# Loading the second chunk's q two tokens to a row and turning it by heads and parity

## The chip, the cores and the metric

The kernel runs on one core of one Trainium2 chip. The metric is the device time of one execution in microseconds (us); smaller is better. Before the change the median of three runs is 208.63 us.

## The reference

Two layers follow each other. The first is a linear attention with decay, in blocks of 64 tokens, over 4 batches, 8 heads, 768 tokens and a head width of 64. The second is a feed-forward layer whose activation is h + sin(alpha h)^2 / alpha, on 3072 tokens of width 512 with an inner width of 2048.

```python
for b in range(nb):                                   # blocks of 64 tokens
    intra = einsum('bhic,bhjc->bhij', qb, kb) * Dmask
    intra = einsum('bhij,bhjd->bhid', intra, vb)
    inter = einsum('bhid,bhde->bhie', qb * lam_pow, kv_state)
    out[:, :, sl] = intra + inter
    kv_state = lam_block * kv_state + einsum('bhsd,bhse->bhde', kb * rev_pow, vb)
x = out.transpose(0, 2, 1, 3).reshape(B * S, H * D)
h = x @ w_in
s = sin(alpha * h)
result = (h + s * s / (alpha + 1e-9)) @ w_out
```

All inputs and the output are fp32; the kernel computes with bf16 operands on TensorE.

## The kernel before

The 768 tokens are cut into six chunks `t` of 128 tokens, each with all four batches, which gives groups `g` of 512 rows for the feed-forward layer. While group `g` goes through the feed-forward layer, the attention of chunk `g + 1` is worked in between. The order of all instructions is written by hand: the program text is the order on every engine. TensorE makes 16 hidden blocks `f` of a group (`hidden`, L461: four matmuls of 512 columns each) and, in units of four matmuls, the second product (`project`, L489). Such units wait in the list `behind` and are put in by `run(n)`. ScalarE computes the sine and mostly the square (L464, L469; for some blocks of group 0 the square is on VectorE, L477). VectorE finishes a block (`finish`, L478).

For the attention of chunk 1, which the change is about, these steps matter:

- Loads. GpSimd issues them; they convert fp32 to bf16. Each row that is read is one token of one head, 64 values. A load puts the 128 tokens on 128 partitions, with 16 rows (two batches times eight heads) side by side on each (`load`, L104). For q and k of batches 2 and 3, the heads of the pair stand one place further (L101 and L102), in two transfers.
- Turning. Scores need q and k with the head width on partitions. `turn` makes four transposes on TensorE for one batch (two heads at a time, L281) into one PSUM bank, and a copy brings them to the tile `QKT`: on ScalarE (L283) or VectorE (L285). k of chunk 1 is turned by `turns_pair` (L295, L298). Later chunks are turned mostly by the DMA.
- `scores` (L397) multiplies turned k and q into two banks, `masks` (L404, VectorE) applies the decay, and `states` (L377) makes the key-value products. `update` adds these to the state on VectorE (L353, L357); GpSimd decays and casts states (L342, L346), and `decay_k` (L242, GpSimd) makes the decayed k.
- `outputs_first` (L411) multiplies q by the state, `outputs` (L436) adds the scores times v, and `leave` (L443, VectorE) writes the attention's result.

Around the first turn of q the text runs as follows. It names the banks in use, which sets what waits for what:

```python
        if f == 13:
            turn(1, "q", 0, 2, V)        # bank 2
            turn(1, "q", 1, 3, V)        # bank 3
        if f == 14:
            scores(1, (0,), (4, 2))      # banks 4 and 2
            masks(1, 0)
        if f == 15:
            run(1)
            states(1, (0,), (4, 2))      # the same banks
```

The second turn of q, for batches 2 and 3, comes after group 0's hidden blocks: into banks 5 and 0, copied by ScalarE, followed by one unit of `project` (the first that reads the third part of w_out) and `scores(1, (1,), (5, 0))`. Banks 5 and 0 hold `outputs_first` of the first pair before, which `leave` reads.

Of the kernel before, what the change touches and what calls it, by code (L numbers as in the profile page):

```python
# [11 lines left out]
BF16 = mybir.dt.bfloat16  # L12
# [3 lines left out]
def kernel(  # L16
# [11 lines left out]
    nc = tc.nc  # L28
    P = nc.NUM_PARTITIONS

    B, H, S, D = q.shape
    T = 128
    NT = S // T
    HP = H // 2
# [23 lines left out]
    def bank(nm, n, dtype=FP32):  # L58
        return psum.tile([P, 512 if dtype is FP32 else 1024], dtype, name=nm, tag=f"b{n}")
# [6 lines left out]
    LO, HI = slice(0, D), slice(D, 2 * D)  # L66
# [4 lines left out]
    qn, kn, vn = {}, {}, {}  # L71
    NAT = {"k": (kn, k), "q": (qn, q), "v": (vn, v)}

    def new_chunk(t):
        for d, nm, p in ((qn, "qn", qkp), (kn, "kn", qkp), (vn, "vn", vp)):
            d[t] = p.tile([P, B, H, D], BF16, name=nm)
# [14 lines left out]
    def load_w_out(i):  # L91
        nc.gpsimd.dma_start(out=w_out_sb[i][:],
                            in_=moe_w_out[i * 512:(i + 1) * 512, :].rearrange("(f p) d -> p f d", p=P))

    def load(t, nm, b0, b1):
        dst, src = NAT[nm]
        to = dst[t][:, b0:b1, :, :].rearrange("p b h e -> p (b h) e")
        by_head = src[b0:b1, :, t * T:(t + 1) * T, :].rearrange("b h p e -> p (b h) e")
        n = H * (b1 - b0)
        if t and nm != "v" and b0 == 2:  # L100
            nc.gpsimd.dma_start(out=to[:, 0:n - 1, :], in_=by_head[:, 1:n, :])  # L101
            nc.gpsimd.dma_start(out=to[:, n - 1:n, :], in_=by_head[:, 0:1, :])  # L102
        else:
            nc.gpsimd.dma_start(out=to, in_=by_head)  # L104

    new_chunk(0)
    new_chunk(1)
# [24 lines left out]
    iden = consts.tile([P, P], BF16, name="iden")  # L132
# [71 lines left out]
    def mask_table():  # L204
        nc.gpsimd.tensor_tensor(
            out=C64[:], in0=tri64[:].unsqueeze(1).unsqueeze(1).broadcast_to([P, 2, HE, D]),
            in1=later["NE64"][:].unsqueeze(3).broadcast_to([P, 2, HE, D]), op=ALU.mult)


    V, G, A = nc.vector, nc.gpsimd, nc.scalar  # L210
    xt = {}
    kdec = {}
    KT, QT, both = {}, {}, {}
# [14 lines left out]
    def home(t, blk):  # L228
        return SB[2 if blk else t % 2]
# [7 lines left out]
    def decay_k(t, b0, b1):  # L237
        if t not in kdec:
            kdec[t] = kdp.tile([P, B, H, D], BF16, name="kdec")
        R = later["R64" if t else "R128"]  # L240
        o = int(turned_by_one(t, b0 // 2))
        nc.gpsimd.tensor_tensor(out=kdec[t][:, b0:b1, :, :], in0=kn[t][:, b0:b1, :, :],  # L242
                                in1=R[:, o:o + H].unsqueeze(1).unsqueeze(3).broadcast_to([P, b1 - b0, H, D]),
                                op=ALU.mult)
# [32 lines left out]
    def turn(t, nm, b, n, eng):  # L277
        src, u = (kn, 0) if nm == "k" else (qn, 1)
        ps = bank("T_ps", n, BF16)[:].rearrange("p (n c i) -> p n c i", n=2, c=HP)[:, u]
        for hp in range(HP):  # L280
            nc.tensor.transpose(out=ps[:, hp, :], in_=src[t][:, b, 2 * hp:2 * hp + 2, :], identity=iden[:])  # L281
        if eng is nc.scalar:
            eng.copy(out=both[t][:, u, b, :, :], in_=ps)  # L283
        else:
            eng.tensor_copy(out=both[t][:, u, b, :, :], in_=ps)  # L285

    def halves(hd):
        return slice(hd * D, (hd + 1) * D)

    def turns_pair(t, nm, b, bk, engines):  # L290
        src, n = (kn, 0) if nm == "k" else (qn, 1)
        ps = bank("T_ps", bk, BF16)[:].rearrange("p (u c i) -> p u c i", u=2, c=HP)
        for u in range(2):
            for hp in range(HP):
                nc.tensor.transpose(out=ps[:, u, hp, :], in_=src[t][:, b + u, 2 * hp:2 * hp + 2, :], identity=iden[:])  # L295
        for u, eng in enumerate(engines):
            if eng is nc.scalar:
                eng.copy(out=both[t][:, n, b + u, :, :], in_=ps[:, u])  # L298
            else:
                eng.tensor_copy(out=both[t][:, n, b + u, :, :], in_=ps[:, u])  # L300

    def scores1(t, b, ns):
        Fb = [bank("F0_ps", n)[:].rearrange("p (c i) -> p c i", c=HP) for n in ns]
        for hp in range(HP):
            for hd in range(2):
                nc.tensor.matmul(out=Fb[hd][:, hp, :], lhsT=KT[t][halves(hd), b, hp, :],
                                 rhs=QT[t][halves(hd), b, hp, :], start=True, stop=True)
        st = work.tile([P, 2, HP, T], BF16, name="STm")
        for hd in range(2):
            nc.vector.tensor_tensor(out=st[:, hd], in0=Fb[hd], in1=C0[:, hd], op=ALU.mult)  # L310
        STm[t, b] = st
# [18 lines left out]
    def states1(t, pr, n):  # L330
        ps = bank("KV0_ps", n)[:].rearrange("p (u c d) -> p u c d", u=2, c=HP)
        for h in range(2 * H):
            half, m = where(1, pr, h)
            nc.tensor.matmul(out=ps[halves(half), m // HP, m % HP, :], lhsT=head(kdec, t, pr, h),
                             rhs=vn[t][:, 2 * pr + h // H, h % H, :], start=True, stop=True)
        new_state(1, pr, ps, "first")
# [4 lines left out]
    def decay_state(n, pr):  # L341
        nc.gpsimd.tensor_tensor(out=pair(SD, pr), in0=pair(S_of[n], pr), op=ALU.mult,  # L342
                                in1=L64[:, pr].unsqueeze(1).unsqueeze(3).broadcast_to([P, 2, HP, D]))

    def cast_state(n, pr, dst):
        nc.gpsimd.tensor_copy(out=pair(dst, pr), in_=pair(S_of[n], pr))  # L346
# [54 lines left out]
    def masks(t, pr):  # L401
        st = work.tile([P, 2, 2, HP, D], BF16, name="STm")
        for hd in range(2):
            nc.vector.tensor_tensor(out=st[:, hd], in0=att["F", t, pr, hd], op=ALU.mult,  # L404
                                    in1=of_mask(C64, t, pr, hd).unsqueeze(1).broadcast_to([P, 2, HP, D]))
        STm[t, pr] = st
# [50 lines left out]
    def hidden(g, f, between=None):  # L457
        hps = bank("hps", H0[f] if g == 0 else (0, 5, 4, 2)[f] if g == 1 and f < 4 else AB[0] if g == 1 and f == 15 else AB[f + 1] if g == 2 and f < 2 else HB[(f + 2) % 3] if g == 1 else HB[(16 * g + f + 1) % 3])
        w = w_in_sb[f // 4]
        for c in range(NDC):  # L460
            nc.tensor.matmul(out=hps[:], lhsT=w[:, c, (f % 4) * P:(f % 4 + 1) * P],  # L461
                             rhs=xt[g][:, c, :], start=(c == 0), stop=(c == NDC - 1))
        s_sb = mlps.tile([P, GRP], BF16, name="s_sb")
        nc.scalar.activation(out=s_sb[:], in_=hps[:], func=ACTF.Sin, scale=alpha_sb[:, f:f + 1])  # L464
        if between:
            between()
        s2 = mlps.tile([P, GRP], BF16, name="s2")
        if squarer(g, f) is A:
            nc.scalar.activation(out=s2[:], in_=s_sb[:], func=ACTF.Square)  # L469
        elif squarer(g, f) is G:  # L470
            nc.gpsimd.tensor_tensor(out=s2[:], in0=s_sb[:], in1=s_sb[:], op=ALU.mult)
        hps_of[g, f] = (hps, s_sb, s2)
# [102 lines left out]
    decay_k(0, 0, 2)  # L575
    decay_k(0, 2, 4)
    mask_table()
    for nm in "kqv":
        load(1, nm, 0, 2)
    load_w_out(1)  # L580
    for nm in "kv":
        load(1, nm, 2, 4)
# [20 lines left out]
    def run(n):  # L603
        for _ in range(min(n, len(behind))):
            behind.pop(0)()
# [3 lines left out]
    for f in range(NFC):  # L609
        hidden(0, f)  # L610
        if f in (1, 10):
            states1(0, f // 10, 2 if f == 10 else 4)
        if f == 10:
            decay_k(1, 0, 2)
            decay_state(1, 0)
            cast_state(1, 0, home(1, 0))
            load(1, "q", 2, 4)
            load_w_out(2)
            load_w_out(3)
            load(2, "v", 0, 2)  # L620
        if f in (11, 12):
            run(1)
        if f == 12:
            turns_pair(1, "k", 0, 4, (A, A))
        if f == 13:
            turn(1, "q", 0, 2, V)
            turn(1, "q", 1, 3, V)
        if f == 14:
            scores(1, (0,), (4, 2))
            masks(1, 0)  # L630
        if f == 15:
            run(1)
            states(1, (0,), (4, 2))
            finish(0, 14)
            update(1, 0, 0)
        if f != 14:
            finish(0, f)
# [3 lines left out]
    update(1, 1, 0)  # L641
    run(2)
    turns_pair(1, "k", 2, 4, (A, A))
    run(1)
    outputs_first(1, (0,), (5, 0))
# [4 lines left out]
    states(1, (1,), (4, 2))  # L650
    update(1, 0, 1)
    run(1)
    turn(1, "q", 2, 5, A)
    turn(1, "q", 3, 0, A)
    load(2, "k", 0, 2)
    run(1)
    update(1, 1, 1)
# [110 lines left out]
```

## Time and profile before

| | before |
|---|---|
| median of 3 runs | 208.63 us (208.5 to 208.82) |
| the profiled execution's own time | 209.41 us |
| its span in the trace | 207.6 us |
| TensorE busy | 198.1 us (95%) |
| VectorE busy | 131.5 us (63%) |
| ScalarE busy | 142.8 us (69%) |
| GpSimd busy | 108.7 us (52%) |

The trace is of one execution. Its times count from the start of the span. In the rows PE is TensorE's matmuls, PEld its weight loads, DVE VectorE, ACT ScalarE and POOL GpSimd. L281 is line 281 of the kernel. A row of the timeline gives the start, the time from the first start to the last end, the engine, the line and the operation, what is written and read with its shape, and the count of instructions merged. In brackets stands the idle time before it, and what ended that. A few matmul records are missing, so a group of four can show as three.

### The profile page before, as it was taken

To read this page: it belongs to the slowest core of one execution; us is meant where nothing else is said; L and a number is where in the kernel's file an instruction comes from. 1 tells how busy PE (TensorE), PEld (TensorE's weight loads), DVE (VectorE), ACT (ScalarE), POOL (GpSimd) and SP (SyncE) were. 2 spreads that over 40 slices of the span, in tenths; PEclk is the share of its full clock that TensorE was granted. 3 is DMA by queue.
4 is the path that set the end of the run, shared out by engine and by line. 5 is a ranking of instruction groups with operands and counts; after the bars stand their busy time and mean duration, and the time that the engine had idled before them with its cause. 6 is when DMAs were issued, how large, how long until landed. Compare 5 with 4: busy or idle time off the path is not lost.

```text
span 207.6 us, 5321 instructions
## 1 busy us (share of the span) xinstructions
PE 198.1 (95%) x2203; PEld 98.7 (48%) x2233; DVE 131.5 (63%) x218; ACT 142.8 (69%) x240; POOL 108.7 (52%) x114
## 2 busy tenths in 40 slices
PE   7996999999999999999999999999999999999993
PEld 2652445564455445444444444444445444444462
DVE  6792898582898969967556957555867544444000
ACT  4895998323989799675776575776666787887121
POOL 8999949998799984999966930002000000000000
PEclk9999999999999999999999999999999999999999
DMA  8999999999999999699999999501101101110212
GB/s 127 148 151 203 197 164 182 175 188 157 124 215 191 150 138 200 51 163 159 109 139 151 181 124 163 143 0 54 51 3 54 51 0 51 52 54 0 101 61 92
DMA packets 98826, 24.47 MB, mean 118 GB/s; under 512 B 91490, under 2 KB 95858, under 8 KB 98802
## 3 DMA queue, kind: packets, MB, share of 16 engines
q0 software_dynamic: 77248, 13.37, 88.7%
q1 hardware_dynamic: 21552, 10.76, 26.9%
q8 instruction: 17, 0.28, 0.6%
q14 instruction: 7, 0.06, 0.1%
q10 hardware_dynamic: 2, 0.00, 0.0%
HBM read 27.27 MB, written 6.29 MB: 162 GB/s over the span
## 4 chain that ended last, share of the span: by engine, by line
PE 67%; DMA 14%; POOL 11%; issue 3%; ACT 3%; DVE 0%; POOLq 0%; ACTq 0%; SPq 0%
PE ops L489 30%; PE hps L461 29%; DMA qn<-in_q_dram 6%; DMA QKT<-qn 5%; DMA w_in<-in_moe_w_in_dram 3%; POOL vn L104 2%; ACT s_sb L464 2%; PE O_ps L411 2%; POOL kn L104 2%; POOL qn L104 2%; PE hps L513 2%; POOL SD L342 2%; PE F_ps L397 1%; POOL sb L346 1%; PE O_ps L436 1%
## 5 line engine op out<-in xcount | busy, mean ns | idle before, releaser
L478 DVE SCALAR_TENSOR_TENSOR gall<-s,r_sb,hps 128x512 bf16<-128x512 bf16 x96 | 71.1, 744 | 45.1 <-ACT s L469 44.9
L461 PE MATMUL hps<-xt,w_in 128*128 128x512 bf16 x369 | 94.4, 379 | 2.8 <-DMA w_in<-in_moe_w_in_dram 1.7
L489 PE MATMUL ops<-w_out,gall 128*128 128x512 bf16 x353 | 90.3, 379 | 1.0 <-issue 0.3
L464 ACT ACTIVATE s_sb<-hps,alpha_sb 128x512 bf16<-128x512 f32 x96 | 65.3, 684 | 33.6 <-PE hps L461 33.1
L469 ACT ACTIVATE s<-s_sb 128x512 bf16<-128x512 bf16 x91 | 57.3, 630 | 2.8
L461 PEld LDWEIGHTS <-w_in 128*128 128x128 bf16 x384 | 36.5, 98 | 44.8 <-DMA w_in<-in_moe_w_in_dram 2.5
L489 PEld LDWEIGHTS <-gall 128*128 128x128 bf16 x368 | 34.8, 98 | 40.6 <-issue 0.8
L242 POOL TENSOR_TENSOR kdec<-kn,R 128x1024 bf16<-128x1024 bf16 x12 | 23.0, 1943 | 5.4 <-DMA kn<-in_k_dram 5.4
L346 POOL CAST sb<-S 128x512 bf16<-128x512 f32 x20 | 12.3, 620 | 20.7 <-DVE S L353 20.7
L342 POOL TENSOR_TENSOR SD<-S,L 128x512 f32<-128x512 f32 x16 | 16.7, 1047 | 6.2 <-DVE S L353 6.0
L443 DVE TENSOR_TENSOR xt<-O_ps,Etab 128x512 bf16<-128x512 f32 x20 | 12.8, 684 | 6.3 <-PE O_ps L436 6.3
L104 POOL DMA_DIRECT2D vn<-in_v_dram x13 | 14.8, 1152 | 0.0
L496 DVE COPY o_sb<-ops 128x512 f32<-128x512 f32 x15 | 10.3, 689 | 4.2 <-PE ops L489 4.1
L404 DVE TENSOR_TENSOR STm<-F_ps,C 128x512 bf16<-128x512 f32 x20 | 12.8, 681 | 0.2 <-PE F_ps L397 0.2
L498 ACT COPY o_sb<-ops 128x512 f32<-128x512 f32 x8 | 4.6, 576 | 12.0 <-PE ops L489 12.0
L353 DVE TENSOR_TENSOR S<-SD,KV_ps 128x512 f32<-128x512 f32 x16 | 10.9, 682 | 0.2 <-POOL SD L342 0.2
L130 PE MATMUL hps<-fill 128*128 128x256 bf16 (+1 forms) x30 | 8.3, 386 | 1.5 <-DVE fill L123 1.5
L104 POOL DMA_DIRECT2D kn<-in_k_dram x8 | 8.8, 1106 | 0.3 <-issue 0.3
L104 POOL DMA_DIRECT2D qn<-in_q_dram x8 | 8.7, 1091 | 0.0
L283 ACT COPY QKT<-T_ps 128x512 bf16<-128x512 bf16 x10 | 5.5, 586 | 3.4 <-PE T_ps L281 3.2
L101 POOL DMA_DIRECT2D qn<-in_q_dram x5 | 6.1, 1221 | 1.3 <-DMA qn<-in_q_dram 1.3
L411 PEld LDWEIGHTS <-sb 64*64 64x64 bf16 x320 | 4.4, 108 | 4.8 <-issue 4.7
(75 smaller groups left out, 114.0 us busy)
## 6 DMA issues: line engine op xcount, KB each, us to landing
out_dram<-o_sb SPq DMA_DIRECT2D x23, 256.0 KB, 2.3
vn<-in_v_dram POOLq DMA_DIRECT2D x10, 256.0 KB, 8.8
w_out<-in_moe_w_out_dram POOLq DMA_DIRECT2D x4, 512.0 KB, 11.0
w_in<-in_moe_w_in_dram POOLq DMA_DIRECT2D x3, 512.0 KB, 10.3
kn<-in_k_dram POOLq DMA_DIRECT2D x5, 256.0 KB, 8.4
qn<-in_q_dram POOLq DMA_DIRECT2D x5, 256.0 KB, 10.1
kn<-in_k_dram POOLq DMA_DIRECT2D x5, 240.0 KB, 8.3
qn<-in_q_dram POOLq DMA_DIRECT2D x5, 240.0 KB, 9.0
```

What stands on the lines that cost most here:

```text
L104: nc.gpsimd.dma_start(out=to, in_=by_head)
L242: nc.gpsimd.tensor_tensor(out=kdec[t][:, b0:b1, :, :], in0=kn[t][:, b0:b1, :, :], in1=R[:, o:o + H].unsqueeze(1).unsqueeze(3).broadcast_to ...
L342: nc.gpsimd.tensor_tensor(out=pair(SD, pr), in0=pair(S_of[n], pr), op=ALU.mult, in1=L64[:, pr].unsqueeze(1).unsqueeze(3).broadcast_to([P, ...
L346: nc.gpsimd.tensor_copy(out=pair(dst, pr), in_=pair(S_of[n], pr))
L353: nc.vector.tensor_tensor(out=S, in0=pair(SD, pr), in1=ps, op=ALU.add)
L404: nc.vector.tensor_tensor(out=st[:, hd], in0=att["F", t, pr, hd], op=ALU.mult, in1=of_mask(C64, t, pr, hd).unsqueeze(1).broadcast_to([P, 2 ...
L443: nc.vector.tensor_tensor(out=xview(t)[:, 2 * pr:2 * pr + 2, blk, :, :], in0=att["O", t, pr, blk], in1=Eb, op=ALU.mult)
L461: nc.tensor.matmul(out=hps[:], lhsT=w[:, c, (f % 4) * P:(f % 4 + 1) * P], rhs=xt[g][:, c, :], start=(c == 0), stop=(c == NDC - 1))
L464: nc.scalar.activation(out=s_sb[:], in_=hps[:], func=ACTF.Sin, scale=alpha_sb[:, f:f + 1])
L469: nc.scalar.activation(out=s2[:], in_=s_sb[:], func=ACTF.Square)
L478: nc.vector.scalar_tensor_tensor(out=gall[g][:, f, :], in0=s2[:], scalar=r_sb[:, f:f + 1], in1=hps[:], op0=ALU.mult, op1=ALU.add)
L489: nc.tensor.matmul(out=ops[:], lhsT=gall[g][:, f, m * P:(m + 1) * P], rhs=w_out_sb[part][:, f % 4, :], start=(f == 0), stop=(f == NFC - 1))
```

## The change

Only q of chunk 1 is touched. A row that is read now holds two neighbouring tokens of a head, 128 values. A batch's 128 tokens lie on 64 partitions: the first batch of a pair on the lower half, the second on the upper half. On each partition are eight heads, each with the even and then the odd token of its pair of tokens. The load of batches 0 and 1 is two transfers instead of one. That of batches 2 and 3 is three instead of two, as the second half is split by the shift of heads.

Turning takes 16 transposes for a pair of batches, one for each head place and parity: 128 partitions and 64 columns go to 64 partitions and 128 columns. The columns of a result are 64 token pairs of the one batch and 64 of the other. All 16 go to one bank, where a pair took two banks before. The heads alternate between the lower and the upper half of the partitions. Then two copies, one for each batch, write tokens back in order: even and odd tokens go to every second element of `QKT`. The first pair's copies are on VectorE and the second pair's on ScalarE, as before.

```diff
+    def in_twos(t, b):
+        return qn[t][:, b:b + 2].rearrange("p b h d -> p (b h d)").rearrange("p (h x) -> p h x", h=H)
+
+    def load_twos(t, b):
+        src = q[b:b + 2, :, t * T:(t + 1) * T, :].rearrange("b h (p e) d -> p (b h) (e d)", e=2)
+        o = int(bool(t) and b == 2)
+        for rows, s0, s1, n in ((LO, 0, H, o), (HI, 0, H - o, H + o), (HI, H - o, H, 0)):
+            if s0 < s1:
+                nc.gpsimd.dma_start(out=in_twos(t, b)[rows, s0:s1, :], in_=src[:, n:n + s1 - s0, :])
...
+    def turn_twos(t, b, bk, engines):
+        ps = bank("T_ps", bk, BF16)[:].rearrange("p (c e n) -> p c e n", c=HP, e=2)
+        for s in range(H):
+            for e in range(2):
+                nc.tensor.transpose(out=ps[halves(s % 2), s // 2, e, :],
+                                    in_=in_twos(t, b)[:, s, e * D:(e + 1) * D], identity=iden[:])
+        for u, eng in enumerate(engines):
+            to = both[t][:, 1, b + u, :, :].rearrange("p c (i e) -> p c e i", e=2)
+            if eng is nc.scalar:
+                eng.copy(out=to, in_=ps[:, :, :, u * D:(u + 1) * D])
+            else:
+                eng.tensor_copy(out=to, in_=ps[:, :, :, u * D:(u + 1) * D])
...
-    for nm in "kqv":
-        load(1, nm, 0, 2)
+    load(1, "k", 0, 2)
+    load_twos(1, 0)
+    load(1, "v", 0, 2)
...
-            load(1, "q", 2, 4)
+            load_twos(1, 2)
...
-            turn(1, "q", 0, 2, V)
-            turn(1, "q", 1, 3, V)
+            turn_twos(1, 0, 2, (V, V))
...
-    turn(1, "q", 2, 5, A)
-    turn(1, "q", 3, 0, A)
+    turn_twos(1, 2, 5, (A, A))
```

## The prediction

> **What bounds the kernel now.** I read the page's head first, then the windows view for the stretch in which chunk 1 is turned, then the timelines of TensorE, VectorE, ScalarE and GpSimd there.
>
> ```profile
> span 207.6 us, 5321 instructions
> PE 198.1 (95%) x2203; PEld 98.7 (48%) x2233; DVE 131.5 (63%) x218; ACT 142.8 (69%) x240; POOL 108.7 (52%) x114
> ```
> ```profile
> 30.00:50.00 20.00, 19.49 (x347) 10.91 (x352) 13.73 (x27) 8.83 (x17) 19.54 (x21) 1.00 1.98 176
> ```
>
> TensorE is busy for 95% of the span, and for 19.49 of the 20 us around the change, at full granted clock (the 1.00). Only 0.51 us of idle time is there to win. So what counts is whether the change lengthens TensorE's stream or puts a wait into it. TensorE's rows around the first turn (q of batches 0 and 1, at hidden block 13):
>
> ```profile
> 31.77 1.03 PE L461 MATMUL hps<-xt,w_in 128*128 128x512 bf16 x3
> 32.63 0.61 PE L281 MATMUL T_ps<-iden,qn 128*128 128x128 bf16 x8
> 33.08 1.03 PE L461 MATMUL hps<-xt,w_in 128*128 128x512 bf16 x4
> 34.03 0.45 PE L397 MATMUL F_ps<-QKT 64*64 64x64 bf16 x32
> 34.41 0.82 PE L461 MATMUL hps<-xt,w_in 128*128 128x512 bf16 x3
> 35.28 1.03 PE L489 MATMUL ops<-w_out,gall 128*128 128x512 bf16 x4
> 36.24 0.45 PE L377 MATMUL KV_ps<-vn,kdec 64*64 64x64 bf16 x32
> 36.62 1.90 PE L489 MATMUL ops<-w_out,gall 128*128 128x512 bf16 x8
> ```
>
> Columns: start, length, engine, line, operation. A group of four 512-column matmuls takes 0.86 us of issue (35.28 to 36.14; "x3" rows lack a record). The groups follow each other without a gap, except that 0.1 us passes before a group of 64-wide tiles (36.14 to 36.24). VectorE in the same stretch, and one earlier row for a price:
>
> ```profile
> 29.29 0.68 DVE L351 COPY S<-KV_ps 128x512 f32<-128x512 f32 x1
> 33.05 0.76 DVE L285 COPY QKT<-T_ps 128x512 bf16<-128x512 bf16 x2 [0.27 <-PE T_ps L281]
> 33.77 0.42 DVE L477 TENSOR_TENSOR s<-s_sb 128x512 bf16<-128x512 bf16 x1
> 34.23 0.75 DVE L478 SCALAR_TENSOR_TENSOR gall<-s,r_sb,hps 128x512 bf16<-128x512 bf16 x1
> 34.89 1.28 DVE L404 TENSOR_TENSOR STm<-F_ps,C 128x512 bf16<-128x512 f32 x2
> ```
>
> From the q copies (L285) to the end of the masks (L404, 36.17) VectorE has no slack: the square and finish of block 13 stand between them. And the key-value products (L377) at 36.24 write the two banks that the masks read. They come 0.07 us after the masks end. So here TensorE is one step ahead of a VectorE chain that is just in time; whatever delays the copies moves TensorE.
>
> **Part 1: the transposes.** Each pair of batches goes from 8 transposes of 128 columns of q to 16 of 64 columns; the identity still streams 128 columns. No row shows a transpose with a 64-column result. The nearest are the 128-wide transposes and L317, which has the same shape (128 rows, 64 result columns, 128 streamed):
>
> ```profile
> L281 PE MATMUL T_ps<-iden,qn x32: 216/219/311, 6.5 to 43.4; 128*128 128x128 bf16 x32
> L317 PE MATMUL O_ps<-STm,vn x32: 219/219/243, 12.7 to 14.8; 128*64 128x128 bf16 x32
> 12.74 0.64 PE L317 MATMUL O_ps<-STm,vn 128*64 128x128 bf16 x16
> 13.31 0.50 PE L130 MATMUL hps<-fill 128*128 128x256 bf16 x3
> ```
>
> Taking the last one's 0.219 us off the group, the 8 transposes start (0.61 - 0.219)/7 = 56 ns apart, and L317's 16 start (0.64 - 0.219)/15 = 28 ns apart: its results alternate between the two halves of the partitions, and two run at once. The next group starts 0.15 us after L317's last start (13.16 to 13.31). The new loop also changes halves, but only after two instructions (the parities) on the same half. If one half works while the other is issued, 28 ns holds on average too. Bounds: 28 and 56 ns. I take 28, the row of the same shape. First turn: start 32.63 + 0.1, last start 0.42 later (33.15), its end 33.37 (high end: 33.57 and 33.79). The next group starts at 33.30 instead of 33.08.
>
> **Part 2: the copies on VectorE.** Both copies now read one bank, so the first waits for all 16 transposes; before, it waited for the first four. It starts at 33.40 instead of 33.05 (the same 0.03 us after the last end). Each still moves 512 elements per partition, but writes every second 2-byte element. No row shows that. The nearest rows are L285 itself (0.42 each, 0.76 for two) and L351, the copy of as many fp32 elements (0.68; two of that length take 1.28, by L404). L285 saves 0.26 us, half a nanosecond an element: it seems to move two neighbours at a time. Outputs two apart are not neighbours, so I take L351's: 1.28 us. It cannot be below 0.76, since no element is saved.
>
> The Trainium skill's page "VectorE: DVE Perf Modes", section "What auto-detection actually checks", says that the paired 16-bit mode needs a step of one in every tensor, and so speaks against this change. By its table in "The TRN2 errata" a 512-element copy out of PSUM would be an estimated 658 ns unpaired and 392 paired; with these the sum would differ by 0.01 us.
>
> Ends: 33.40 + 1.28 = 34.68 instead of 33.81, so 0.87 late. The square, finish and masks follow, all 0.87 later; masks end at 37.04, and L377 starts at 37.11 instead of 36.24: **0.87 us**. TensorE's own path asks for less: scores (L397) wait for the copies until about 34.73 instead of 34.03 (0.70), so L377 would be there at 36.94 and wait 0.17 for the masks. Low end, paired copies: 0.35. High end, 56 ns: 1.29. Behind L377 everything on TensorE moves with it.
>
> **Part 3: the second turn** (q of batches 2 and 3):
>
> ```profile
> 39.76 0.69 PE L411 MATMUL O_ps<-QKT,sb 64*64 64x64 bf16 x31
> 42.92 0.68 PE L281 MATMUL T_ps<-iden,qn 128*128 128x128 bf16 x8
> 43.63 1.02 PE L489 MATMUL ops<-w_out,gall 128*128 128x512 bf16 x4
> 44.59 0.55 PE L397 MATMUL F_ps<-QKT 64*64 64x64 bf16 x32
> 44.95 0.78 PE L411 MATMUL O_ps<-QKT,sb 64*64 64x64 bf16 x31
> 43.34 1.07 ACT L283 COPY QKT<-T_ps 128x512 bf16<-128x512 bf16 x2 [2.65 <-PE T_ps L281]
> 43.89 1.12 DVE L357 SCALAR_TENSOR_TENSOR S<-S,L,KV_ps 128x128 f32<-128x128 f32 x4
> ```
>
> In the old times: transposes from 43.02, last start 43.44, so the next group can start at 43.59, no later than now (43.63): the 8 took 0.71 us from start to the next group, 0.26 more than in the first turn, since the second four waited for bank 0. The new form uses bank 5 only. But both ScalarE copies now wait for the last transpose: 43.69 instead of 43.34. Two take 1.07, which I keep (low and high end alike, as ScalarE's copies are 0.58 whether they write 2 or 4 bytes by the row below), until 44.76. Scores write bank 5 and must wait for both, to 44.80 instead of 44.59: 0.21 late. Of this 0.09 comes back, since L411 behind them takes 0.78 here and 0.69 at 39.76, held by the state update (L357, until 45.01), which will be done. Net **0.12 us**; with 56 ns, 0.54.
>
> ```profile
> 49.82 0.58 ACT L498 COPY o_sb<-ops 128x512 f32<-128x512 f32 x1 [3.81 <-PE ops L489]
> ```
>
> **Part 4: the loads.** Rows of the queue and of landing times (first issue of q at 21.37; then w_out 2; then w_out 0):
>
> ```profile
> 21.37 1.25 POOL L104 DMA_DIRECT2D qn<-in_q_dram  x1
> 30.46 1.89 POOL L242 TENSOR_TENSOR kdec<-kn,R 128x1024 bf16<-128x1024 bf16 x1 [3.02 <-DMA kn<-in_k_dram]
> 33.86 1.26 POOL L101 DMA_DIRECT2D qn<-in_q_dram  x1
> 35.11 0.58 POOL L102 DMA_DIRECT2D qn<-in_q_dram  x1
> DMA to landing us min/median/max: 10.2/10.5/10.8
> DMA to landing us min/median/max: 7.9/7.9/7.9
> DMA to landing us min/median/max: 13.9/13.9/13.9
> ```
> ```profile
> DMA packets 2458, 0.31 MB, mean 156 GB/s; under 512 B 2458, under 2 KB 2458, under 8 KB 2458
> DMA packets 828, 0.82 MB, mean 206 GB/s; under 512 B 23, under 2 KB 828, under 8 KB 828
> ```
>
> The first of these two windows (28 to 30 us) is q, k and v: 128-byte packets, 2 x 16/2458 us = 13.0 ns of an engine each. The second (19 to 23) is 1-KB weight rows, 77 ns each. Between them 256 bytes cost 22 ns: q of two batches falls from 2048 x 13.0/16 = 1.67 us to 1024 x 22/16 = 1.41. That is 0.26 us a load (none if bytes alone count, 0.83 if packets alone do), and TensorE sees none of it: q lands at 21.37 + 10.8 = 32.17 and is used at 32.63. GpSimd issues one transfer more each time. By L101 and L102 (1.26 for 15 rows per partition, 0.58 for one) a half of 64 partitions and 8 rows is about 0.7: 1.4 instead of 1.25, then 2.0 instead of 1.84. The first is hidden in the 3.02 us in which L242 waits for k. In the program the transfers take turns on eight semaphores, so one more moves the last v load behind w_out 0's landing, 28.4 us; it ends by 29.6, still ahead of L242. If that cover fails, it costs what passes 30.46. The second 0.2 us lies ahead of a state cast that will itself come later with TensorE. I cost both at nothing.
>
> **Sum.** 0.87 + 0.12 = 0.99 us. Against the profiled execution: span 207.6 to 208.6, its own time 209.41 to 210.4; that run lies 0.78 above the median 208.63 of three, so the median goes to 209.6. Bounds: 0.35 + 0.12 = 0.47, so 209.1; 1.29 + 0.54 = 1.83, so 210.5.
>
> **Rivals.**
> - Paired copies: VectorE keeps 0.42 a copy with every second element written. For it: nothing but the equal count; against it: the 0.26 that L285 saves needs an explanation. 209.1.
> - Transposes one by one, 56 ns: two in a row on the same half block the next pair. For it: L317 alternates every instruction, this doesn't. 210.5.
> - Late q: 64 partitions reach only half of the DMA engines. Then 1024 x 22/8 = 2.8 us instead of 1.67, q lands at 33.3, transposes start 0.6 to 0.7 later than the 32.73 above: 1.65 in all, 210.3. Against it: nothing in the trace splits engines by partition. It decides once q lands after 32.7.
> - Faster: the shorter loads free TensorE from waits on the queue. w_out 2 lands at 35.67 + 7.9 = 43.57, and L489 starts on it at 43.63 though the transposes were all issued by 43.4. If that and the rest of the 0.51 us of idle time went, and transposes and copies came no later, 208.1. It decides only if copies come less than about 0.1 us late; the sixteen starts and the shared bank speak against that. If the loads' packets don't grow at all, the first forecast stands, since it takes nothing from them.
>
> **How the numbers follow.** This kernel's times can be told apart by about 0.2%, 0.42 us. Chances: the sum 0.52; paired copies 0.18 (0.05 of it within 0.2%, as 209.1 is near the edge of 209.05); one by one 0.14; late q 0.07; relief 0.09 (0.06 faster, 0.03 within). Slower 0.86, same 0.08, faster 0.06. The range runs from 209.0 (below paired copies) to 210.4 (late q and part of one by one); it leaves out relief and the far end of one by one.
>
> **What would show it.** Right: 16 transposes whose last starts 0.42 us after the first; VectorE copies of 0.68; masks ending 0.9 later relative to block 13; L377 waiting for them; scores of the second turn 0.2 late; no load row on TensorE's waits. Wrong: copies of 0.42, starts 56 ns apart, a wait of the first transposes for q, or TensorE's lost time made up behind 45 us, where I see no slack.

## The result and the profile after

| | before | with the change |
|---|---|---|
| median | 208.72 us (6 runs, 208.44 to 209.07) | 209.97 us (6 runs, 209.37 to 210.74) |
| ratio to before | | 1.0056, 95% interval 1.0032 to 1.0081 |
| ratio when run again with the experiments | | 1.0038, 1.0019 to 1.0057 |
| the profiled execution's own time | 209.41 us | 209.37 us |
| its span | 207.6 us | 207.6 us |

Two comparisons put the change 0.6% and 0.4% slower, about 1.2 and 0.8 us. The two traced executions have the same span all the same: the one of before, 209.41 us, is slower than all six runs in the table, and the one with the change is the fastest of its six. So the traces must be compared by stages, not by their ends. Two later traces, of the loads alone and of the repeated change, were taken at a granted clock of 0.56 and 0.66 and are left aside. TensorE's rows of the changed kernel around the two turns of q (L316 the transposes, L420 scores, L400 key-value products, L434 `outputs_first`, L484 hidden blocks, L512 `project`):

```profile
31.00 1.03 PE L484 MATMUL hps<-xt,w_in 128*128 128x512 bf16 x4
31.96 0.64 PE L316 MATMUL T_ps<-iden,qn 128*64 128x128 bf16 x16
32.53 1.04 PE L484 MATMUL hps<-xt,w_in 128*128 128x512 bf16 x4
33.52 0.19 PE L420 MATMUL F_ps<-QKT 64*64 64x64 bf16 x1
34.04 0.44 PE L420 MATMUL F_ps<-QKT 64*64 64x64 bf16 x31 [0.33 <-DVE QKT L323]
36.24 0.51 PE L400 MATMUL KV_ps<-vn,kdec 64*64 64x64 bf16 x32
43.09 0.64 PE L316 MATMUL T_ps<-iden,qn 128*64 128x128 bf16 x16
43.78 1.02 PE L512 MATMUL ops<-w_out,gall 128*128 128x512 bf16 x4
45.15 0.45 PE L420 MATMUL F_ps<-QKT 64*64 64x64 bf16 x32 [0.34 <-ACT QKT L321]
45.43 0.67 PE L434 MATMUL O_ps<-QKT,sb 64*64 64x64 bf16 x31
51.72 1.03 PE L512 MATMUL ops<-w_out,gall 128*128 128x512 bf16 x4
```

And the copies on VectorE and ScalarE with what follows the first pair, from the timelines:

```profile
32.65 1.34 DVE L323 COPY QKT<-T_ps 128x512 bf16<-128x512 bf16 x2 [0.62 <-PE T_ps L316]
33.88 0.40 DVE L500 TENSOR_TENSOR s<-s_sb 128x512 bf16<-128x512 bf16 x1
34.98 1.28 DVE L427 TENSOR_TENSOR STm<-F_ps,C 128x512 bf16<-128x512 f32 x2
43.77 1.33 ACT L321 COPY QKT<-T_ps 128x512 bf16<-128x512 bf16 x2 [3.01 <-PE T_ps L316]
```

In the changed trace two rows now name a wait of the scores for a copy (34.04 and 45.15). From the start of hidden block 13 to the key-value products it takes 36.24 - 31.00 = 5.24 us; before it took 36.24 - 31.77 = 4.47. That is 0.77 more. From there to the `project` group between the hidden blocks of group 1 it takes 15.48 (to 51.72), before 15.11 (to 51.35, the row below): 0.37 more. Of this, 0.07 lies in the key-value products themselves: the next group follows 0.45 after their start (36.69), before 0.38. I call the whole stretch, 19.58 us before and 20.72 after, **the stage**. It is 1.14 us longer.

Two things outside the stage give that back in these two traces. The first weights let TensorE go on at 17.50 instead of 18.27. And in chunk 4 the unchanged kernel waited for a turn by the DMA, which the changed one did not. Rows of before, then of after:

```profile
18.27 1.04 PE L461 MATMUL hps<-xt,w_in 128*128 128x512 bf16 x4 [1.72 <-DMA w_in<-in_moe_w_in_dram]
51.35 1.03 PE L489 MATMUL ops<-w_out,gall 128*128 128x512 bf16 x4
116.22 0.45 PE L397 MATMUL F_ps<-QKT 64*64 64x64 bf16 x32
116.89 0.45 PE L397 MATMUL F_ps<-QKT 64*64 64x64 bf16 x32 [0.23 <-DMA QKT<-qn]
117.27 1.04 PE L489 MATMUL ops<-w_out,gall 128*128 128x512 bf16 x3
```
```profile
17.50 1.04 PE L484 MATMUL hps<-xt,w_in 128*128 128x512 bf16 x4 [1.19 <-DMA w_in<-in_moe_w_in_dram]
116.58 0.74 PE L420 MATMUL F_ps<-QKT 64*64 64x64 bf16 x64
117.25 1.04 PE L512 MATMUL ops<-w_out,gall 128*128 128x512 bf16 x4
```

The first of the two lies ahead of every changed instruction. It scatters: in the twelve traces compared here, hidden block 13 began between 30.99 and 31.80 us. The second is not there every time: a second trace of the kernel before, from the experiments below, has no such wait:

```profile
31.54 1.03 PE L461 MATMUL hps<-xt,w_in 128*128 128x512 bf16 x3
51.47 1.03 PE L489 MATMUL ops<-w_out,gall 128*128 128x512 bf16 x4
116.33 0.74 PE L397 MATMUL F_ps<-QKT 64*64 64x64 bf16 x64
117.00 1.04 PE L489 MATMUL ops<-w_out,gall 128*128 128x512 bf16 x3
```

Its stage is longer, 19.93 us. But from block 13 to the `project` unit behind these scores both traces of the kernel before take the same, 85.50 (to 117.27) and 85.46 (to 117.00), and the change takes 86.25 (to 117.25). So the 1.14 us of the stage is the larger of two readings. Against the second trace the stage is 0.79 us longer, and over the longer stretch the change costs 0.75 to 0.79.

### The profile page after: what moved, and what is told of

Its sections match the earlier page's. It is cut to its first block, busy times and chain, and to the rows that moved or that the text cites. A ratio compares the mean times of both kernels' runs of the same rounds, so it can differ in the third digit from the quotient of the medians.

```text
span 207.6 us, 5386 instructions
## 1 busy us (share of the span) xinstructions
PE 199.6 (96%) x2249; PEld 97.9 (47%) x2249; DVE 132.0 (64%) x218; ACT 143.1 (69%) x240; POOL 109.3 (53%) x116
## 4 chain that ended last, share of the span: by engine, by line
PE 89%; POOL 5%; DMA 3%; ACT 1%; issue 1%; DVE 0%; POOLq 0%; ACTq 0%
PE hps L484 40%; PE ops L512 39%; DMA w_in<-in_moe_w_in_dram 3%; PE O_ps L434 2%; PE F_ps L420 2%; PE hps L536 2%; PE KV_ps L400 2%; POOL kn L104 1%; PE O_ps L459 1%; POOL qn L104 1%; POOL vn L104 1%; POOL vn L126 1%; PE T_ps L305 1%; ACT QKT L321 1%; PE T_ps L316 1%
## 5 line engine op out<-in xcount | busy, mean ns | idle before, releaser
L484 PE MATMUL hps<-xt,w_in 128*128 128x512 bf16 x384 | 95.9, 379 | 1.3 <-DMA w_in<-in_moe_w_in_dram 1.2
L512 PE MATMUL ops<-w_out,gall 128*128 128x512 bf16 x368 | 92.1, 379 | 0.1
L487 ACT ACTIVATE s_sb<-hps,alpha_sb 128x512 bf16<-128x512 f32 x96 | 65.3, 685 | 33.3 <-PE hps L484 33.1
L484 PEld LDWEIGHTS <-w_in 128*128 128x128 bf16 x384 | 36.5, 98 | 44.4 <-DMA w_in<-in_moe_w_in_dram 2.0
L512 PEld LDWEIGHTS <-gall 128*128 128x128 bf16 x368 | 34.8, 98 | 40.6 <-issue 0.6
L140 PE MATMUL hps<-fill 128*128 128x256 bf16 (+1 forms) x30 | 7.6, 360 | 1.5 <-DVE fill L133 1.5
L104 POOL DMA_DIRECT2D kn<-in_k_dram x8 | 8.8, 1101 | 0.3 <-issue 0.3
L104 POOL DMA_DIRECT2D qn<-in_q_dram x7 | 7.4, 1062 | 0.0
L434 PEld LDWEIGHTS <-sb 64*64 64x64 bf16 x320 | 4.3, 108 | 4.8 <-issue 4.2
L101 POOL DMA_DIRECT2D kn<-in_k_dram x5 | 6.3, 1258 | 0.0
L434 PE MATMUL O_ps<-QKT,sb 64*64 64x64 bf16 x320 | 5.7, 195 | 0.0
```

The source lines that it names most:

```text
L434: nc.tensor.matmul(out=att["O", t, pr, blk][halves(h % 2), u, h // 2, :], lhsT=home(t, blk)[halves(half), 2 * pr + m // HP, m % HP, :], rh ...
L512: nc.tensor.matmul(out=ops[:], lhsT=gall[g][:, f, m * P:(m + 1) * P], rhs=w_out_sb[part][:, f % 4, :], start=(f == 0), stop=(f == NFC - 1))
```

## The experiments

All were compared with the kernel before in the same session. "Stage" is as above, from one trace each; that of the loads alone is from their second trace. With the loads alone, the turning alone or dense copies, the tokens of chunk 1's q end up in another order, so these kernels show times only.

| edit | ratio, 95% interval | stage, us |
|---|---|---|
| the kernel before again | 0.9997, 0.9974 to 1.0020 | 19.93 |
| the loads of the change alone | 1.0059, 1.0032 to 1.0085 | 20.84 |
| the turning of the change alone | 1.0052, 1.0027 to 1.0078 | 20.73 |
| the change, dense copies | 1.0046, 1.0023 to 1.0069 | 21.00 |
| the loads alone, v later | 0.9988, 0.9964 to 1.0011 | 20.02 |
| the change, dense copies, v later | 1.0019, 0.9993 to 1.0045 | 20.19 |
| the change, v later | 1.0043, 1.0015 to 1.0072 | 20.72 |
| the change in two banks, v later | 1.0017, 0.9993 to 1.0042 | 20.35 |
| the kernel before, v later | 0.9995, 0.9976 to 1.0013 | 20.20 |
| the kernel before, TensorE 0.76 us late | 1.0019, 0.9998 to 1.0040 | 20.35 |

**Loads or turning.** The first theory was that the turning costs the time and the loads cost nothing; the rival, that GpSimd's additional transfers do.

```diff
 # loads alone: the change, but
-            turn_twos(1, 0, 2, (V, V))
+            turn(1, "q", 0, 2, V)
+            turn(1, "q", 1, 3, V)
-    turn_twos(1, 2, 5, (A, A))
+    turn(1, "q", 2, 5, A)
+    turn(1, "q", 3, 0, A)
 # turning alone: the change, but
-    load_twos(1, 0)
+    load(1, "q", 0, 2)
-            load_twos(1, 2)
+            load(1, "q", 2, 4)
```

> Only the loads of the change; q is turned as before, from 64-partition rows, so the tokens and batches of chunk 1's q are mixed up in its result. Stage measured: from the first matmul of hidden block 13 to the project group behind the two hidden blocks of group 1, 19.58 us before (31.77 to 51.35), 20.72 with the change (31.00 to 51.72). If the turning and its copies cost the time: stage 19.4 to 19.6, whole 208.4 to 208.8. If the loads do (one more transfer each time on GpSimd, v held back behind the weights): stage above 20.2, whole above 209.3.

> Only the turning of the change; q is loaded as before, so its tokens are mixed up in the result. If the turning and its copies cost the time: stage 20.6 to 20.8, whole 209.7 to 210.1. If the loads do: stage 19.6 to 19.9, whole below 209.1.

The turning alone costs all that the change costs (stage 20.73), as expected. But so do the loads alone: 1.0059, against my expectation. The new theory was tested on a second trace of the loads alone:

> The loads alone once more (token order of chunk 1's q wrong), for a trace at full clock. New theory: the extra transfer makes GpSimd wait for an earlier transfer ahead of the second chunk's v load, and the state casts behind it come late. Then the first cast behind that load starts 0.7 to 1.1 us later than 38.28 - 31.77 = 6.51 after hidden block 13, O_ps waits for it, and the stage is 20.0 to 20.4 instead of 19.58. If GpSimd has slack, as I predicted: 19.4 to 19.6.

TensorE and GpSimd of that trace, from the timelines:

```profile
32.51 0.61 PE L291 MATMUL T_ps<-iden,qn 128*128 128x128 bf16 x8 [0.19 <-DMA qn<-in_q_dram]
36.83 1.90 PE L512 MATMUL ops<-w_out,gall 128*128 128x512 bf16 x8
44.62 0.41 PE L420 MATMUL F_ps<-QKT 64*64 64x64 bf16 x21
45.75 0.28 PE L420 MATMUL F_ps<-QKT 64*64 64x64 bf16 x11 [0.72 <-issue]
45.84 0.67 PE L434 MATMUL O_ps<-QKT,sb 64*64 64x64 bf16 x31
```
```profile
28.21 1.16 POOL L104 DMA_DIRECT2D vn<-in_v_dram  x1 [1.71 <-DMA w_out<-in_moe_w_out_dram]
39.21 0.63 POOL L369 CAST sb<-S 128x512 bf16<-128x512 f32 x1
44.96 0.62 POOL L369 CAST sb<-S 128x512 bf16<-128x512 f32 x1
```

The new theory held in part: the casts are late, but not in the place that I named. The first cast behind the v load is 7.91 us after hidden block 13 (39.21 - 31.30; expected 7.2 to 7.6, before 6.51), but `outputs_first` of the first pair did not wait for it, as it starts at 39.97. The next cast, at 44.96, ends at 45.58, and `outputs_first` of the second pair needs it: it starts at 45.84, instead of right behind the scores. Why the last eleven score products stop with it, the profile doesn't name. The first turn also waited 0.35 us for q (32.51 instead of 32.16). So the stage, 20.84, is above the expected 20.0 to 20.4, and the casts are only part of it: of the 1.26 us over 19.58, 0.58 lies behind the key-value products (15.31 us from 36.83 to the end of the stage, before 14.73) and 0.68 ahead of that, where q was late.

**The v loads moved.** To take the casts away as a cause, the two v loads of chunk 2 that stand ahead of them are issued later.

```diff
-            load(2, "v", 0, 2)            # behind the w_out loads, hidden block 10
...
-    load(2, "v", 2, 4)
+    load(2, "v", 0, 2)
...
+    load(2, "v", 2, 4)                    # behind update(1, 0, 1)
     load(2, "k", 0, 2)
```

> The loads alone (token order wrong), with the two v loads of chunk 2 issued later: the first where the second stood, the second behind the state update of the second pair. If the casts behind the first v load are what the loads cost: no wait of O_ps for a cast, stage back to 19.4 to 19.6, whole within 0.2% of before. If the loads cost in another way: stage as in the run without this move, whole 0.4% above before.

> The whole change, only with the two v loads of chunk 2 later. If late casts and late copies are two chains side by side, of which the later one counts, then taking the casts away alone leaves the copies: stage 20.5 to 20.7 us, whole 0.3 to 0.5% above before. If they add up: stage 19.6 to 20.0, whole within 0.2% of before.

> The kernel before with only the two v loads of chunk 2 issued later. If GpSimd's casts held TensorE a little even before (O_ps at 44.95 took 0.78 instead of 0.69): ratio 0.998 to 1.000, stage 19.4 to 19.6. If they had slack: ratio 1.000, stage 19.6 to 19.9.

With the loads alone the move takes the cost away: 0.9988. The stage is 20.02; what is left over 19.58 lies in the first turn, where VectorE's chain was late, and in no cast: behind the key-value products it takes 14.72 us, before 14.73. This execution began late, with block 13 at 31.76, and did not wait for q, so its stage shows the casts gone and no late q. The fall of the ratio, from 1.0059 to 0.9988, is larger than 0.58 us; for the rest the traces do not account. On the whole change the move takes little or nothing: 1.0043, stage 20.72. So the loads' late casts and the turning's late copies lie side by side, and only the later one counts; they don't add. On the kernel before the move does nothing that these runs can tell: 0.9995. Its stage of 20.20 was longer than I expected either way, and its row says why (kernel before, v later):

```profile
43.75 0.59 PE L489 MATMUL ops<-w_out,gall 128*128 128x512 bf16 x2 [0.82 <-DMA w_out<-in_moe_w_out_dram]
```

Here hidden block 13 began early, at 31.07, and TensorE then waited at the first use of w_out's third part.

**Dense copies.** The copies write neighbours, which leaves the tokens in another order.

```diff
-            to = both[t][:, 1, b + u, :, :].rearrange("p c (i e) -> p c e i", e=2)
+            to = both[t][:, 1, b + u, :, :].rearrange("p c (e i) -> p c e i", e=2)
```

> The change with the four copies writing neighbours: even and odd tokens stay apart, so the token order of chunk 1's turned q is wrong. If the copies' length is the main cost: VectorE's copies fall from 0.72 to 0.42 and ScalarE's from 0.74 to 0.58, and the stage from 20.7 to 20.0 to 20.2 us, whole about 209.2 to 209.4. If the sixteen transposes on TensorE are: stage 20.6 to 20.7, whole unchanged against the change.

> The change with dense copies (token order wrong) and the two v loads of chunk 2 later. If the dense copies saved time on TensorE's stream and the late casts took it back: stage 20.0 to 20.3 instead of 21.00 with dense copies alone, and 20.72 for the change. If it stays above 20.6, copies and casts are not the cause.

The copies' rows, of the change first and of dense copies then (the lines' view: minimum, median and maximum in ns):

```profile
L323 DVE COPY QKT<-T_ps x2: 708/720/731, 32.6 to 33.3; 128x512 bf16<-128x512 bf16 x2
L321 ACT COPY QKT<-T_ps x2: 736/736/736, 43.8 to 44.4; 128x512 bf16<-128x512 bf16 x2
```
```profile
L323 DVE COPY QKT<-T_ps x2: 415/420/424, 32.6 to 33.0; 128x512 bf16<-128x512 bf16 x2
L321 ACT COPY QKT<-T_ps x2: 585/588/592, 43.9 to 44.4; 128x512 bf16<-128x512 bf16 x2
```

Dense copies alone did not help: the stage is 21.00 instead of the expected 20.0 to 20.2, though each copy is as short as foreseen. The trace names the casts in their place (dense copies):

```profile
39.62 1.00 PE L434 MATMUL O_ps<-QKT,sb 64*64 64x64 bf16 x31
45.70 0.66 PE L434 MATMUL O_ps<-QKT,sb 64*64 64x64 bf16 x30 [0.23 <-POOL sb L369]
```

With the v loads moved as well, the stage falls to 20.19, inside the expected 20.0 to 20.3, and the ratio to 1.0019. So with the copies short, the casts come last; with both short, little is left. The ratios of these runs overlap (1.0019 here, 1.0043 with long copies and the v loads later), so this order rests on the stages and on the wait named above.

**Two banks.** The transposes are split by heads into two halves with a bank and a copy each, so that the first copy needs eight transposes only. The tokens are in order here.

```diff
-        ps = bank("T_ps", bk, BF16)[:].rearrange("p (c e n) -> p c e n", c=HP, e=2)
-        for s in range(H):
+        for part, eng in enumerate(engines):
+            ps = bank("T_ps", bk[part], BF16)[:].rearrange("p (c e u i) -> p c e u i", c=HP, e=2, u=2)
+            cs = slice(2 * part, 2 * part + 2)
+            for s in range(HP * part, HP * (part + 1)):
...
-            turn_twos(1, 0, 2, (V, V))
+            turn_twos(1, 0, (2, 3), (V, V))
-    turn_twos(1, 2, 5, (A, A))
+    turn_twos(1, 2, (5, 0), (A, A))
```

> The change with the sixteen transposes in two halves by heads, each with its own bank and its own copy of both batches (second elements still written apart), and the v loads later. The first copy no longer waits for all sixteen. If copies in series behind the last transpose are the cost: first copies start 0.2 earlier, stage 20.2 to 20.5, whole 0.1 to 0.4% above before. If only their length counts: stage as with the v loads moved alone.

Stage 20.35 and ratio 1.0017, as expected. This is the best complete version that loads two tokens to a row; it is no faster than the kernel before.

**Repeats, and a delay alone.**

> The changed kernel again. The stage should repeat at 20.7 us within 0.1. The beginning should not: the first traces of before and after reached hidden block 13 at 31.77 and 31.00, and the change touches nothing ahead of it on TensorE, so I expect another value here between 30.9 and 32.0. Whole 209.4 to 210.5.

> The kernel before, run as if it were a change. If the difference of 0.4 to 0.6% that all four variants showed comes from the kernels, this one gives a ratio within 0.2% of 1 and a stage of 19.5 to 19.7 us; if it comes from the comparison, a ratio near 1.005. The first hidden block's second part begins somewhere between 17.4 and 18.4 us, as the first weights land.

The change repeats at 1.0038; it has no second stage to compare. The kernel before repeats at 0.9997, so the comparison has no offset of its own. Its stage, 19.93, was above the 19.5 to 19.7 that I expected: the stage scatters by some 0.3 us even there. The last experiment asks how much of a delay ahead of w_out's third part is paid:

```diff
         if f == 13:
+            spin(7, 3)
             turn(1, "q", 0, 2, V)
```

> The kernel before with seven idle matmuls of 256 columns (0.76 us, results unused) ahead of the first turn of q: it delays TensorE and the chain behind it by about what the first turn's copies cost, and changes no load and no copy. New theory: TensorE meets the third part of w_out in the unit behind the second turn, and that lands at 43.5 to 43.75 in nearly all traces, so of a delay ahead of it only what exceeds TensorE's wait there is paid. Then the unit starts at the later of the landing and its own time (31.0 to 31.8 for hidden block 13, plus 12.43), and the whole costs less than the 0.76: 0 to 0.5 us, a ratio of 1.000 to 1.0025. If nothing takes it up: 0.76 us, 1.0036.

The ratio is 1.0019, some 0.4 us, but the interval reaches from nothing to the whole 0.76, so the ratio does not settle it. Of its trace, w_out's third part (the first of the two transfers in the first row) and the unit that reads it:

```profile
35.81 1.50 POOL L92 DMA_DIRECT2D w_out<-in_moe_w_out_dram  x2
DMA to landing us min/median/max: 8.5/8.5/8.5
44.34 1.02 PE L489 MATMUL ops<-w_out,gall 128*128 128x512 bf16 x4
```

The load landed at 35.81 + 8.5 = 44.31, later than the 43.5 to 43.75 that I had counted on, and the unit started right behind it. So here the wait at the load took up nothing. Block 13 began at 31.80, and the stage of 20.35 is 0.77 us over the first trace of the kernel before and 0.42 over the second. What an average execution pays stays open.

## Why the prediction was right, and where its steps were off

The forecast was 209.6 (209.0 to 210.4), slower; measured were 209.97 and, against the same kernel before, 0.8 to 1.2 us more. Its sum of 0.99 stands beside 1.14 in the traces' stage, and 0.79 against the second trace of the kernel before. The first turn came out a little below its term and the second well above it, so part of the closeness of the sum is luck.

- **Sixteen transposes.** Right. They start (0.64 - 0.219)/15 = 28 ns apart on average in both turns, the next group follows 0.57 us after the first start in the first turn (0.69 in the second, where it comes right behind a landing, see below), and the rival of one by one (56 ns) is out.
- **VectorE's copies.** Right in kind: unpaired, 0.72 each, 1.34 for two, with 0.68 and 1.28 forecast. With 0.42 for dense copies of the same data, the step of two is the cause. This agrees with the Trainium skill's rule ("VectorE: DVE Perf Modes", "What auto-detection actually checks"); the estimate of 658 ns from that page's table was 62 ns short. The rival of paired copies is out.
- **First turn, 0.87.** Measured 0.77 to the start of the key-value products and 0.84 to the group behind them. The masks end at 36.26, 5.26 after block 13 instead of 4.40, so VectorE's chain is 0.86 late, as forecast. But the key-value products did not wait to start until the masks ended. TensorE's own path, with the scores waiting for the copies, brought them to 36.24, and they then took 0.51 instead of 0.45. In the second trace of the kernel before they took 0.69 without any change, so this chain scatters by itself.
- **Second turn, 0.12.** Undersized: 0.30, from the group behind the key-value products to the end of the stage (15.03 instead of 14.73). I kept ScalarE's copy at 0.58, since fp32 output was no slower. But with every second element written it takes 0.74, and two take 1.33 instead of 1.07. The scores started 1.37 after the unit before them instead of 0.96. The part that came back behind them was larger than the 0.09.
- **The old second turn.** Part 3 put its 0.71 us down to a wait for bank 0. Only 0.07 of it lies among the transposes (0.68 instead of 0.61 in the first turn). The unit behind them starts at 43.63, just behind the landing of w_out's third part at 35.67 + 7.9 = 43.57, as the relief rival has it. With the change the load lands at 35.70 + 8.0 = 43.70 and the unit starts at 43.78. So in both traces this landing, and not the transposes, sets the unit's start.
- **Loads at nothing.** True for the whole change, where the turning is later; wrong as a statement about GpSimd. I named the v load that would wait for w_out 0 (it did, until 27.93), and missed that the next v load would wait too. The changed kernel's GpSimd timeline:

```profile
27.93 1.16 POOL L104 DMA_DIRECT2D vn<-in_v_dram  x1 [1.40 <-DMA w_out<-in_moe_w_out_dram]
37.85 1.16 POOL L104 DMA_DIRECT2D vn<-in_v_dram  x1 [0.60 <-DMA kn<-in_k_dram]
39.00 0.63 POOL L369 CAST sb<-S 128x512 bf16<-128x512 f32 x1
44.75 0.62 POOL L369 CAST sb<-S 128x512 bf16<-128x512 f32 x1
```

The cast at 44.75 ends at 45.37, and `outputs_first` starts at 45.43. The cover I had named, that TensorE comes later too, was there with 0.06 us to spare. Without it the loads cost as much as the turning.

- **Late q and relief.** The loads alone met q 0.35 late once, in an early execution; the changed kernel's trace did not: there q's two transfers land 9.3 and 9.6 us after their issue, the later at about 31.6, ahead of the 32.17 of before. In no trace with these loads did q land after 32.5, so the late-q rival, with a landing at 33.3, is out; the wait of 0.35 is smaller than the 0.6 that it named. The relief rival's row was real: w_out's third part (w_out 2) lands 7.9 us after its issue before and 8.0 with the change, so the change won nothing there. But the wait for it takes up part of a delay when an execution starts early. How much of the 1.14 us is taken up in an average execution, the runs do not settle, as only traced ones show where they started.

## What to carry to other kernels

A load that packs more into a row moves the reordering to the engines behind it: look first at what the copy out of PSUM costs with its new step, on each engine that makes it, and at which work stands in that engine's queue behind it. One more transfer on a queue that takes turns on a few semaphores can hold later ones back, so count the transfers between each load and the one whose place it takes. When two parts of a change each cost the whole, they can lie side by side: an experiment that removes one shows nothing until the other is removed as well.

## What the runs showed of the hardware that was not expected

ScalarE's copy of 512 bf16 elements out of PSUM takes 0.74 us when it writes every second element and 0.58 when it writes neighbours. Transposes into 64 partitions keep their 28 ns on average even when two in a row go to the same half. And with the v loads later, w_out 2 landed 6.8 to 7.3 us after its issue in the four traces with the two-token loads, and 8.7 in the one trace with the old loads. The old loads' issue was also earlier (35.02 instead of 35.73 to 36.33), so how much of this the longer rows give is not shown. TensorE had little use for it.
